# A new hand-written order of all engines in a linear-attention and GEGLU block

## The chip, the cores and the metric

One Trainium2 chip, one of its cores. The time is the device time of one execution in microseconds; the time of the kernel before is the median of three such runs. Beside them stands one execution under the hardware profiler, whose span runs from its first to its last instruction.

## The reference

The input `x` has 2048 rows of 640 numbers in bf16. A layer norm is followed by a linear attention of 32 heads of 20 numbers with learned softmax features, and, after a residual sum, a second layer norm by a gated feed-forward of 1536.

```python
qkv = layernorm(x) @ wqkv                       # heads of 20
pq, pk = q @ w_phi[h], k @ w_phi[h]
phi_q = concat(softmax(pq), softmax(-pq))       # the same for k
kv = einsum("bhsf,bhsd->bhfd", phi_k, v)
z  = phi_k summed over the rows
o  = (phi_q @ kv) / (phi_q @ z + 1e-6)
h  = x + o @ wo
out = h + (gelu(layernorm(h) @ w_gate) * (layernorm(h) @ w_up)) @ w_down
```

## The kernel before, in words

The rows are 16 tiles of 128, in four blocks of four. Tensor engine (TensorE, PE) products run in bf16 into PSUM, which is handed out as four slots of two banks each (`gtile` takes the slot that was given back first, `give` gives it back; both in the order of the program text, so that a call's slot, and the call whose end it must wait for, follow from the order of the calls).

**Every engine executes its instructions in the order in which the calls stand in the list at the end of the kernel** (from line 687 on, 868 calls). The list is written out by hand: each call, such as `km(3)`, issues the instructions of one step for one tile on one engine or two, and the framework adds only the waits that the data, the buffers and the slots need. So a call that waits holds up everything behind it on its own engine. The change touches this list alone. Each of VectorE (DVE), ScalarE (ACT) and GpSimd (POOL) takes the calls that carry its letter, `"v"`, `"a"`, `"g"`; DMAs are all issued by SyncE (SP), in one queue.

The steps, with their lines:

- Start: `warm` and `warms` (L324, L328) are products of zeros, 512 and 128 columns wide. `load_x`, `load_v`, `load_phi`, `load_w` are plain loads; `load_T(i, d)` (L169) loads a 128-column chunk of the q weights (i = 0) or the k weights (i = 1) transposed.
- Layer norm: for tiles 0 to 2 `c_sum` (L226, L228), `c_xc` (x minus its mean, L235), `c_sq`, `c_rstd`; for the others `bn` in two halves (L265, L267), `rt` (reciprocal root, on ACT or POOL), `mr`, and `ap` (L292 on ACT, L294 on DVE), which writes the normalized tile into one of three buffers. `ap(0)`, `ap(1)`, `ap(2)` write these tiles again with their scale, for q.
- Transposed tiles `LN1T`: `tr` (five PE transposes, L151) and `tc_` (copy out of PSUM, L131) for tiles 0 to 5, `dt` (a DMA transpose, L314) for the others and, a second time, for 0 to 2, which may overwrite the tile only when `km` has read it.
- Weights folded with the feature matrix: `bd` makes a block-diagonal matrix BD, `fm(i, d)` (L367) multiplies and `fc` copies (L131).
- v: `vm` (ten products, L341) and `ve` (L348). k: `km` (ten products, L388) and `ke` (two exponentials, L395). `ks` sums an exponential's features over each head (L404), `kr` takes reciprocals (L408), `kx(t, s, e)` multiplies v by them (L414), and `kv(t)` adds 40 small products, 32 columns wide, into the sums `kvp` (L429).
- When all 16 `kv` are in, `kv_mask` (L439, L442) and `kv_clear(5)` make KV. `qm(j)` (L457) and `qe(j, s)` (L461) make q's features for one or two of 20 column groups: j = 0, 1, 2 and 4 to 7 hold two, j = 3 and 8 to 12 one.
- Per tile: `ab` (40 small products, L502), `ae` (copy, L131), `a_den`, `a_rec`, `a_w`, `a_o` (L535, L538), a transpose (`o_tr` and `o_tc` for tiles 0 and 1, `o_dt` for the rest), `po_` (ten products, L557), `res` (residual, L567 or L578), `sq2`, `rt2`, `ap2`, and a transpose (`tr2` and `tc2`, or `dt2`).
- Feed-forward, per block and slice f of 128 of the 1536: `gu` (ten products, L630), `gl` (gelu, L636), `gm` (L643); then per tile `dn` (two halves of 12 products, L655), `da` (L665), `so` (store, L672). Block 0 is done in two halves of 256 columns.

Of the kernel before, what the change touches and what calls it, by code (L numbers as in the profile page):

```python
# [17 lines left out]
def kernel(  # L18
# [667 lines left out]
    nc.scalar.add_instruction(mybir.InstLoadActFuncSet(name=nc.get_next_instruction_name(), act_func_set_id=6))  # L686
    load_x(0, 1)
# [14 lines left out]
    load_x(8, 10)  # L702
    load_x(12, 14)
    load_x(10, 12)
    warm(1, 0)
    warm(0, 1)
    warm(1, 2)
    warm(1, 3)
    warm(1, 4)
    warm(0, 5)  # L710
    warm(1, 6)
    warms(0, 0)
    warms(0, 1)
    warms(1, 2)
    warms(0, 3)
    warms(0, 4)
    warms(0, 5)
    warms(0, 6)
    warms(1, 7)
    warms(0, 8)  # L720
    warms(1, 9)
    warms(0, 10)
    warms(1, 11)
    warm(1, 7)
    warm(1, 8)
    warm(0, 9)
    c_sum(1, "v")
    c_sum(0, "a")
    c_sq(0)
    c_sq(1)  # L730
    c_sum(2, "a")
    c_xc(0)
    tr(0)
    c_xc(1)
    tr(1)
    tc_(0, 0, 2, "v")
    vm(0, 0, 2)
    tc_(0, 2, 5, "v")
    tc_(1, 0, 5, "v")
    vm(1, 0, 2)  # L740
    vm(1, 2, 4)
    c_xc(2)
    tr(2)
    vm(0, 2, 4)
    vm(1, 4, 5)
    vm(0, 4, 5)
    bn(3, 0)
    bn(3, 1)
    tc_(2, 0, 5, "v")
    vm(2)  # L750
    kv_clear(0)
    bd(0, 3, "g")
    kv_clear(1)
    c_rstd(0, 2)
    c_sq(2)
    bd(3, 5, "g")
    rt(3, 1, "a")
    c_rstd(2, 3)
    ve(1)
    ve(0)  # L760
    bn(5, 0)
    ap(3, "v")
    tr(3)
    bn(5, 1)
    rt(5, 1, "g")
    kv_clear(2)
    kv_clear(3)
    warmed()
    tc_(3, 0, 5, "v")
    ve(2)  # L770
    bn(4, 0)
    bn(4, 1)
    fm(1, 0)
    fm(1, 1)
    fc(1, 1, "v")
    fc(1, 0, "a")
    rt(4, 1, "a")
    ap(4, "v")
    vm(3)
    ve(3)  # L780
    fm(1, 2)
    fc(1, 2, "v")
    fm(1, 3)
    fc(1, 3, "a")
    tr(4)
    ap(5, "v")
    tc_(4, 0, 5, "v")
    fm(1, 4)
    loop_pools()
    fc(1, 4, "a")  # L790
    km(0, True)
    ke(0, 0)
    ke(0, 1)
    km(1)
    ke(1, 0)
    km(3)
    ke(3, 0)
    tr(5)
    tc_(5, 0, 5, "a")
    ke(1, 1)  # L800
    km(4)
    ke(4, 0)
    ke(3, 1)
    bn(7, 0)
    bn(7, 1)
    rt(7, 1, "g")
    bn(6, 0)
    bn(6, 1)
    rt(6, 1, "g")
    bn(8, 0, 2)  # L810
    ap(7, "v")
    dt(7)
    bn(9, 0, 2)
    bn(8, 1, 2)
    ap(6, "v")
    dt(6)
    bn(9, 1, 2)
    rt(8, 2, "g")
    mr(8)
    mr(9)  # L820
    ap(9, "a")
    c_late(0, 3)
    kv_clear(4)
    vm(4)
    ke(4, 1)
    km(2)
    ke(2, 0)
    ve(4)
    vm(5, by_chunk=False)
    ve(5)  # L830
    ke(2, 1)
    ks(0)
    bn(10, 0, 2)
    bn(10, 1, 2)
    kr(0)
    bn(11, 0, 2)
    bn(11, 1, 2)
    rt(10, 2, "g")
    mr(11)
    mr(10)  # L840
    ap(10, "a")
    load_w("g", 2, 3)
    load_x(14, 16)
    ks(1)
    bn(12, 0, 2)
    bn(12, 1, 2)
    kr(1)
    kx(0, 1, "g")
    ap(8, "a")
    vm(7, by_chunk=False)  # L850
    vm(6, by_chunk=False)
    ve(7)
    km(5)
    ke(5, 0)
    ve(6)
    km(6)
    ke(6, 0)
    ke(5, 1)
    ke(6, 1)
    kx(1, 0, "g")  # L860
    kx(1, 1, "g")
    km(7)
    ke(7, 0)
    dt(9)
    load_T(0, 1)
    load_T(0, 3)
    vm(9, by_chunk=False)
    ve(9)
    ke(7, 1)
    fm(0, 3)  # L870
    fc(0, 3, "a")
    km(9)
    kv(1)
    bn(13, 0, 2)
    bn(14, 0, 2)
    bn(13, 1, 2)
    rt(12, 2, "g")
    ap(0, "v")
    ks(2)
    kr(2)  # L880
    ks(3)
# [703 lines left out]
```

## Time and profile before

| | us |
|---|---|
| median of 3 runs | 276.25 (275.69 to 276.27) |
| the profiled execution, its own time | 276.97 |
| span of the profiled execution | 275.3 |
| first v product (L341) | 5.86 |
| first k product (L388) | 14.62 |
| first and last visit to the k^T v sums (L429) | 34.70, 70.32 |
| first `ab` | 73.32 |
| first gelu-stage product (L630) | 91.00 |

In the timeline a line gives the start, the length, the engine and line, the operation, the tile written and read, the shape, and the count of like instructions in a row; in brackets stands how long the engine stood idle before it, and what released it. A visit is a run of `kv` calls that follow each other on PE. In the lines by group, the two numbers after the bar are busy time and mean nanoseconds of one instruction. In the chain that ended last, a piece is its start, its length, and what it was.

### The profile page before, as it was taken

How to read it: one execution, taken by the hardware profiler on the slowest of the kernel's cores; microseconds unless marked ns; L12 is line 12 of the kernel's file. 1: busy time of each engine (PE TensorE's matmuls, PEld its weight loads, DVE VectorE, ACT ScalarE, POOL GpSimd, SP SyncE). 2: the span in 40 equal slices, each digit the busy share in tenths (PEclk: the TensorE clock that was granted, in tenths of full speed). 3: DMA queues.
4: the chain of work that ended last, by engine and by line, in shares of the span. 5: the costliest groups of instructions: out<-in, count | busy, mean ns of one | idle time of the engine just before them, and what ended most of it. 6: DMA issues, size and time to landing. Idle time of an engine off the chain costs nothing.

```text
span 275.3 us, 7091 instructions
## 1 busy us (share of the span) xinstructions
PE 268.4 (98%) x2960; PEld 170.6 (62%) x2977; DVE 174.0 (63%) x316; ACT 138.6 (50%) x241; POOL 90.0 (33%) x195
## 2 busy tenths in 40 slices
PE   8999999999999999999999999999999999999995
PEld 3776766765555887788764544675544576444574
DVE  4879999999487777686584764882375412332413
ACT  6888978784798847346614244622123540213200
POOL 4625978988003032155420221450050140000000
PEclk9999999999999999999999999999999999999999
DMA  7957999750460115211412103152000512020012
GB/s 213 183 183 188 165 231 155 125 146 2 143 247 2 26 27 120 50 27 24 73 26 48 29 21 73 26 105 67 0 13 10 74 34 61 14 84 1 0 38 83
DMA packets 43392, 21.62 MB, mean 79 GB/s; under 512 B 35936, under 2 KB 41312, under 8 KB 43360
## 3 DMA queue, kind: packets, MB, share of 16 engines
q1 hardware_dynamic: 43360, 21.17, 34.4%
q8 instruction: 23, 0.38, 0.6%
q14 instruction: 9, 0.07, 0.1%
HBM read 10.18 MB, written 2.62 MB: 47 GB/s over the span
## 4 chain that ended last, share of the span: by engine, by line
PE 82%; DVE 7%; SPq 4%; DMA 4%; issue 1%; POOL 1%; ACT 0%; DVEq 0%
PE gu L630 38%; PE pd L655 19%; PE pq L457 8%; PE po L557 8%; PE pk L388 3%; DVE stats L265 2%; SPq L169 2%; PE ab L502 2%; DMA WqT<-in_A_wqkv_dram 2%; DVE sk L404 2%; DMA x_sb<-in_A_x_dram 2%; PE kvp L429 2%; PE pv L341 1%; DVE ln L294 1%; POOL vt L414 1%
## 5 line engine op out<-in xcount | busy, mean ns | idle before, releaser
L643 DVE TENSOR_TENSOR GT<-gu,g 128x512 bf16<-128x512 f32 (+1 forms) x60 | 33.2, 579 | 50.6 <-ACT g L636 50.4
L636 ACT ACTIVATE g<-gu 128x512 bf16<-128x512 f32 (+1 forms) x60 | 29.4, 510 | 66.4 <-PE gu L630 65.5
L630 PE MATMUL gu<-LN2T,Wg 128*128 128x512 bf16 (+1 forms) x290 | 61.3, 335 | 0.5
L630 PE MATMUL gu<-LN2T,Wu 128*128 128x512 bf16 (+1 forms) x300 | 61.7, 336 | 0.0
L655 PE MATMUL pd<-Wd,GT 128*128 128x320 bf16 (+2 forms) x396 | 54.0, 295 | 0.0
L655 PEld LDWEIGHTS <-GT 128*128 128x128 bf16 x396 | 37.7, 98 | 14.3 <-DVE GT L643 0.3
L630 PEld LDWEIGHTS <-Wu 128*128 128x128 bf16 x300 | 29.4, 98 | 22.6
L630 PEld LDWEIGHTS <-Wg 128*128 128x128 bf16 x300 | 28.8, 98 | 21.3
L414 POOL TENSOR_TENSOR vt<-vS,rs 128x672 bf16<-128x672 bf16 x24 | 33.4, 1417 | 3.7 <-DVE rs L408 3.7
L665 DVE TENSOR_TENSOR y<-pd,x_sb 128x640 bf16<-128x640 f32 (+3 forms) x18 | 13.3, 741 | 23.4 <-PE pd L655 23.4
L535 DVE TENSOR_TENSOR tt<-AB,w 128x1280 bf16<-128x1280 f32 x16 | 24.0, 1498 | 2.3 <-POOL w L529 2.1
L341 PE MATMUL pv<-Wv,LN1T 128*128 128x320 bf16 x160 | 24.0, 299 | 0.3 <-ACT E L395 0.2
L557 PE MATMUL po<-Wo,oT 128*128 128x320 bf16 x160 | 24.0, 299 | 0.0
L388 PE MATMUL pk<-Wk,LN1T 128*128 128x320 bf16 x160 | 23.5, 299 | 0.2 <-DMA LN1T<-ln 0.2
L457 PE MATMUL pq<-LN1T,Wq 128*128 128x512 bf16 x93 | 22.9, 380 | 0.4
L461 ACT ACTIVATE Eq<-pq 128x1024 bf16<-128x1024 f32 (+1 forms) x26 | 20.3, 839 | 5.6 <-PE pq L457 5.5
L404 DVE TENSOR_REDUCE sk<-E 128x64 f32<-128x1280 bf16 x16 | 23.1, 1447 | 0.0
L131 ACT COPY AB<-ab 128x704 f32<-128x704 f32 x21 | 15.1, 744 | 14.4 <-PE ab L502 10.0
L557 PEld LDWEIGHTS <-oT 128*128 128x128 bf16 x160 | 15.6, 98 | 6.9 <-ACT oT L131 0.2
L341 PEld LDWEIGHTS <-LN1T 128*128 128x128 bf16 x160 | 15.2, 98 | 6.9 <-DVE LN1T L131 0.9
L388 PEld LDWEIGHTS <-LN1T 128*128 128x128 bf16 x160 | 15.3, 98 | 6.3 <-DMA LN1T<-ln 0.4
L395 ACT ACTIVATE E<-pk 128x640 bf16<-128x640 f32 x26 | 17.3, 717 | 3.2 <-PE pk L388 3.2
(104 smaller groups left out, 270.9 us busy)
## 6 DMA issues: line engine op xcount, KB each, us to landing
out_dram<-y SPq DMA_DIRECT2D x15, 160.0 KB, 1.9
x_sb<-in_A_x_dram SPq DMA_DIRECT2D x6, 320.0 KB, 4.9
Wg<-in_B_w_gate_dram SPq DMA_DIRECT2D x5, 384.0 KB, 5.6
Wu<-in_B_w_up_dram SPq DMA_DIRECT2D x5, 384.0 KB, 5.3
Wd<-in_B_w_down_dram SPq DMA_DIRECT2D x4, 480.0 KB, 4.5
x_sb<-in_A_x_dram SPq DMA_DIRECT2D x4, 160.0 KB, 3.0
Wv<-in_A_wqkv_dram SPq DMA_DIRECT2D x2, 320.0 KB
Wo<-in_A_wo_dram SPq DMA_DIRECT2D x1, 480.0 KB, 6.5
```

The lines of the kernel that those rows point to most:

```text
L341: nc.tensor.matmul(pv[t][:, u, 0:HD], lhsT=lnT(t, c), rhs=Wv[:, c, u * HD:(u + 1) * HD], start=(c == 0), stop=(c == NC - 1))
L388: nc.tensor.matmul(pk[t][:, u, 0:HD], lhsT=lnT(t, c), rhs=Wk2[:, c, u * HD:(u + 1) * HD], start=(c == 0), stop=(c == NC - 1))
L404: nc.vector.reduce_sum(sk[t], Ek[t].rearrange("p s (h f) -> p (s h) f", f=Dh), axis=AX.X)
L414: E[e].tensor_tensor(Vt[t][:, s], vS[t % 8], rs[t][:, s * H:(s + 1) * H, None].to_broadcast([P, H, VC]), ALU.mult)
L457: nc.tensor.matmul(pqs[j][:, i, :], lhsT=Wq2[:, kc, c * P:(c + 1) * P], rhs=LN1T[b][:, kc, :], start=(kc == 0), stop=(kc == NC - 1))
L461: nc.scalar.activation(Eq[j][:, :, s, :], pqs[j][:, 0:len(QG[j])], ACTF.Exp, scale=(1.0, -1.0)[s])
L535: nc.vector.tensor_tensor(tt.rearrange("p s (h f) -> p s h f", f=Dh), num, w[t][:, :, :, None].to_broadcast([P, 2, H, Dh]), ALU.mult)
L557: nc.tensor.matmul(po[t][:, u, 0:HD], lhsT=oT[t][:, c, :], rhs=Wo[:, c, u * HD:(u + 1) * HD], start=(c == 0), stop=(c == NC - 1))
L630: nc.tensor.matmul(p[:, i, 0:a1 - a0], lhsT=W[:, c, f * P:(f + 1) * P], rhs=LN2T[b][:, c, a0:a1], start=(c == 0), stop=(c == NC - 1))
L636: nc.scalar.activation(x[:, 0:a1 - a0], p[:, 0, 0:a1 - a0], ACTF.Gelu_apprx_tanh)
L643: nc.vector.tensor_tensor(GT[b, f][:, a0:a1], p[:, 1, 0:a1 - a0], x[:, 0:a1 - a0], ALU.mult)
L655: nc.tensor.matmul(pd[k][:, u, n0:n1], lhsT=GT[b, f][:, tl * P:(tl + 1) * P], rhs=Wd[:, f, u * HD + n0:u * HD + n1], start=(f == 0), stop= ...
```

## The change

The list of calls is written anew; the functions stay as they are. Both lists have 868 calls. PE does the same products in both, but for the zeros at the start (seven long and four short before, six and eight after). What differs besides the order is the engine of some calls. For the part up to the last `kv`: on DVE instead of ACT `c_sum(0)`, `c_sum(2)`, `fc(1, 0)`, `fc(0, 4)` and the copy of tile 5; on ACT instead of DVE `c_sum(1)` and the copies of tiles 0, 2, 3 and 4; on DVE instead of POOL `kx(1, 1)`, `kx(8, 0)`, `kx(10, 0)`, `kx(13, 0)` and `bd(3, 5)`; on POOL instead of DVE `kx(2, 0)` and `kx(13, 1)`. Behind it, some `ae`, `a_den` and `a_w` change engines in both directions, and `o_tc(1)` goes from ACT to DVE.

The diff replaces nearly every line of the list. Cut to the parts that matter here, several calls on one line:

```diff
@@ start, warming products and PE's first calls @@
-warm(1, 0) warm(1, 2) warm(1, 3) warm(1, 4) warm(1, 6) warms(1, 2) warms(1, 7) warms(1, 9) warms(1, 11) warm(1, 7) warm(1, 8)
-c_sum(1, "v") c_sum(0, "a") c_sq(0) c_sq(1) c_sum(2, "a") c_xc(0) tr(0) c_xc(1) tr(1)
-tc_(0, 0, 2, "v") vm(0, 0, 2) tc_(0, 2, 5, "v") tc_(1, 0, 5, "v") vm(1, 0, 2) vm(1, 2, 4) c_xc(2) tr(2)
-vm(0, 2, 4) vm(1, 4, 5) vm(0, 4, 5) bn(3, 0) bn(3, 1) tc_(2, 0, 5, "v") vm(2)
...
-ve(1) ve(0) bn(5, 0) ap(3, "v") tr(3) bn(5, 1) rt(5, 1, "g")
...
-fm(1, 0) fm(1, 1) fc(1, 1, "v") fc(1, 0, "a") rt(4, 1, "a") ap(4, "v") vm(3) ve(3) fm(1, 2) fc(1, 2, "v") fm(1, 3) fc(1, 3, "a")
-tr(4) ap(5, "v") tc_(4, 0, 5, "v") fm(1, 4) loop_pools() fc(1, 4, "a") km(0, True)
+warm(1, 0) warm(1, 2) warm(1, 3) warm(1, 4) warm(1, 5) warm(1, 6) warms(1, 0) warms(1, 1) warms(1, 4) warms(1, 5) warms(1, 6)
...
+c_sum(0, "v") c_xc(0) warms(1, 7) warms(1, 8) tr(0) warms(1, 11) c_sum(1, "a") c_sq(0) c_sq(1) c_xc(1) tr(1)
+tc_(1, 0, 5, "v") vm(1, 0, 2) tc_(0, 0, 2, "a") tc_(0, 2, 5, "a") c_rstd(0, 2) vm(0, 0, 2) vm(0, 2, 4) bd(0, 3, "g")
+c_sum(2, "v") c_xc(2) bn(3, 0) bn(3, 1) rt(3, 1, "a") ap(3, "v") warmed() vm(1, 2, 4) vm(1, 4, 5) ve(1) tr(3)
+tc_(3, 0, 5, "a") bd(3, 5, "v") bn(5, 0) bn(5, 1) vm(0, 4, 5) fm(1, 0) fc(1, 0, "v") rt(5, 1, "g") ap(5, "v")
+bn(4, 0) bn(4, 1) tr(2) tc_(2, 0, 5, "a") ve(0) vm(3) fm(1, 2) tr(5) tc_(5, 0, 5, "v") fc(1, 2, "v")
+c_sq(2) c_rstd(2, 3) c_late(0, 3) ve(3) vm(2) ve(2) rt(4, 1, "a") fm(1, 1) fm(1, 3) fc(1, 1, "v") fc(1, 3, "a")
+ap(0, "v") vm(5, by_chunk=False) fm(1, 4) fc(1, 4, "a") km(0, True) ap(4, "v") tr(4)
@@ loop, DVE's and POOL's calls up to the first kv @@
-bn(8, 0, 2) ap(7, "v") dt(7) bn(9, 0, 2) bn(8, 1, 2) ap(6, "v") dt(6) bn(9, 1, 2)
...
-ks(0) bn(10, 0, 2) bn(10, 1, 2) kr(0) bn(11, 0, 2) bn(11, 1, 2)
...
-ks(1) bn(12, 0, 2) bn(12, 1, 2) kr(1) kx(0, 1, "g")
+ap(6, "v") load_x(8, 10) bn(8, 0, 2) bn(9, 0, 2) rt(7, 1, "g") ap(7, "v") bn(9, 1, 2) bn(8, 1, 2) rt(8, 2, "g") mr(9) ks(0) kr(0) kx(0, 0, "g") mr(8)
+load_x(14, 16) load_x(10, 12) bn(10, 0, 2) load_x(12, 14) bn(12, 0, 2) bn(13, 0, 2) bn(13, 1, 2) dt(0) bn(12, 1, 2) kv_clear(0) rt(12, 2, "g")
...
+bn(11, 0, 2) bn(11, 1, 2) bn(10, 1, 2)
...
+ks(1)
...
+bn(14, 0, 2) ap(13, "v")
...
+kr(1) kx(1, 0, "g") kx(1, 1, "v")
...
+kx(0, 1, "g") kv(0) kv(1)
@@ SP's calls in the loop @@
-load_x(6, 8) load_x(8, 10) load_x(12, 14) load_x(10, 12) dt(7) dt(6) load_w("g", 2, 3) load_x(14, 16) dt(9) load_T(0, 1) load_T(0, 3)
-load_w("u", 1, 2) dt(10) dt(8) dt(0) load_T(0, 0) load_w("g", 3, 4) load_w("g", 0, 1) load_w("o", 2, 5) dt(13) dt(12) dt(11)
-load_w("u", 0, 1) load_T(0, 2) dt(14) load_T(0, 4) load_w("o", 0, 2) dt(1) dt(2) dt(15) load_w("g", 4, 5) load_w("u", 3, 4)
+load_x(6, 8) load_x(8, 10) load_x(14, 16) load_x(10, 12) load_x(12, 14) dt(0) dt(6) dt(7) load_T(0, 4) load_w("g", 0, 1) dt(9) dt(8)
+load_T(0, 0) load_w("u", 1, 2) dt(13) dt(10) dt(12) load_w("u", 2, 3) load_T(0, 1) load_T(0, 2) load_T(0, 3) dt(11) load_w("u", 4, 5)
+load_w("o", 2, 5) load_w("g", 4, 5) dt(14) dt(15) load_w("o", 0, 2) load_w("g", 1, 2) load_w("g", 2, 3) load_w("u", 3, 4) dt(1) dt(2)
+load_w("g", 3, 4) load_w("u", 0, 1)
@@ the visits to the sums: what stands between them on PE @@
-kv(1) kv(0) | kv(3) | kv(2) kv(4) | kv(5) kv(6) kv(7) | kv(12) kv(9) kv(10) | kv(8) kv(14) kv(13) | kv(11) kv(15)
+kv(0) kv(1) | kv(2) kv(3) | kv(4) kv(5) kv(7) | kv(9) kv(12) | kv(14) kv(6) kv(13) kv(10) | kv(15) kv(11) kv(8)
@@ the end of the loop @@
-qm(3) qe(3, 0) qe(3, 1) kx(11, 0, "v") kv(11) kx(15, 1, "v") kv(15) kv_mask(0) kv_mask(2) kv_clear(5) qm(4) qe(4, 1)
-ffn_pools() load_w("d", 0, 3) load_w("d", 9, 12) load_w("g", 1, 2) load_w("d", 3, 6) load_w("u", 4, 5) load_w("u", 2, 3) kv_mask(1) ab(0)
+qm(0) qe(0, 0) qe(0, 1) qm(2) qe(2, 1) ks(15) kr(15) kx(15, 0, "v") kx(8, 0, "v") kx(15, 1, "v") kx(8, 1, "g") kv(15) kx(11, 0, "v") kv(11) kv(8)
+kv_mask(0) kv_mask(1) kv_mask(2) ffn_pools() qm(8) qe(2, 0) kv_clear(5) qe(8, 1) ab(0)
@@ the loads of the down weights @@
+ab(4) ae(4, 1, "a") ae(4, 0, "a") a_rec(3) a_w(3, "v") a_o(3) o_dt(2) load_w("d", 3, 6) load_w("d", 6, 9) o_dt(3) load_w("d", 9, 12) load_w("d", 0, 3)
@@ the end @@
-dn(14, 0) da(14, 0, 2) so(14, 0, 640) dn(15, 1, 0, 192) da(15, 1, 2, 0, 192) so(15, 320, 512) dn(15, 1, 192, 320) da(15, 1, 2, 192, 320) so(15, 512, 640)
+dn(14, 0) dn(15, 1, 0, 192) da(14, 0, 2) da(15, 1, 2, 0, 192) so(13, 0, 640) so(14, 0, 640) so(15, 320, 512)
```

More of the change, by code (lines that the diff above doesn't have):

```diff
@@ L1107 @@
     tc2(1, "v")
-    qe(9, 0)
+    a_rec(2)
+    a_w(2, "g")
+    a_o(2)
+    qe(11, 0)
     qm(12)
```

1304 lines of the change are left out of this document (650 added, 654 removed).

## The prediction

> **What bounds the kernel now.** I read the page first, then the waits of TensorE (PE), then the timelines of PE, VectorE (DVE), ScalarE (ACT), GpSimd (POOL) and SyncE (SP), and last the chain that ended last.
>
> ```profile
> span 275.3 us, 7091 instructions
> PE 268.4 (98%) x2960; PEld 170.6 (62%) x2977; DVE 174.0 (63%) x316; ACT 138.6 (50%) x241; POOL 90.0 (33%) x195
> ...
> PE 82%; DVE 7%; SPq 4%; DMA 4%; issue 1%; POOL 1%; ACT 0%; DVEq 0%
> ```
>
> PE is the bound. Its work is the same in both orders, so the change can win only time in which PE stands still, and lose by making it stand still. The waits of PE after its first instruction are these, and from the first gelu product to the last down product there are none:
>
> ```profile
> PE kvp L429 <- POOL vt L414: 0.4, 1, 0.4
> PE wa L367 <- DMA WqT<-in_A_wqkv_dram: 0.4, 1, 0.4
> PE wa L367 <- ACT vS L348: 0.3, 1, 0.3
> PE pk L388 <- DMA LN1T<-ln: 0.2, 1, 0.2
> PE pv L341 <- ACT E L395: 0.2, 1, 0.2
> ```
> ```profile
> 91.00:272.40 181.40, 180.83 (x1606) 113.72 (x1616) 96.71 (x174) 65.47 (x122) 38.19 (x104) 1.00 0.20 43
> ```
>
> That row is of the view by windows: stretch, its length, then the busy time of PE, 180.83 of 181.40. So after 91 us nothing is to be won. What can be won lies in the start and the loop, and it is little.
>
> **The start, step by step.** The timeline of PE up to the first k product (L388), then of DVE and ACT:
>
> ```profile
> 1.24 2.31 PE L324 MATMUL wu<-zero 128*128 128x512 bf16 x5 [1.24 <-DVE zero L679]
> 3.35 0.63 PE L328 MATMUL wu<-zero 128*128 128x128 bf16 x4
> ...
> 5.86 1.92 PE L341 MATMUL pv<-Wv,LN1T 128*128 128x320 bf16 x12
> ...
> 7.90 2.79 PE L341 MATMUL pv<-Wv,LN1T 128*128 128x320 bf16 x18
> 10.52 0.44 PE L151 MATMUL tp<-ident,ln 128*128 128x128 bf16 x5
> 11.24 0.79 PE L367 MATMUL wa<-BD,WkT 128*128 128x140 bf16 x12 [0.28 <-ACT vS L348]
> ...
> 14.62 1.66 PE L388 MATMUL pk<-Wk,LN1T 128*128 128x320 bf16 x11
> ```
> ```profile
> 3.59 0.82 DVE L228 TENSOR_REDUCE tsum<-x_sb 128x1 f32<-128x640 bf16 x1 [1.26 <-DMA x_sb<-in_A_x_dram]
> 7.61 0.89 DVE L265 BATCH_NORM_STATS2 stats<-x_sb 128x6 f32<-128x320 bf16 x2 [0.34 <-DMA x_sb<-in_A_x_dram]
> ...
> 9.56 0.54 DVE L294 TENSOR_SCALAR ln<-x_sb,mv,rstd 128x640 bf16<-128x640 bf16 x1
> ```
> ```profile
> 4.94 0.83 ACT L239 ACTIVATE junk<-x_sb,tsum 128x640 bf16<-128x640 bf16 x1
> ...
> 8.78 0.29 ACT L275 ACTIVATE ve<-mv,eps 128x1 f32<-128x1 f32 x1 [0.69 <-DVE mv L267]
> 9.11 0.20 ACT L276 ACTIVATE rstd<-ve 128x1 f32<-128x1 f32 x1
> ```
>
> A warming product of 512 columns takes 0.42 (five from 1.24 to 3.35), one of 128 takes 0.11, a real one of 320 takes 0.136 (eleven in 1.66, of which the last shows 0.30). In the new order tr(0) stands behind six long and seven short warming products: 1.24 + 2.53 + 0.77 = 4.5. tr(1) ends at 5.7, DVE copies it (0.47) by 6.4, and the first v product runs at 6.45 instead of 5.86. The copies of tile 0 are now on ACT behind one sum and two squares of about 0.95 each, from 3.6 on: 6.4, and 0.35 for the first part, which the v products of tile 1 cover. 18 products are then done at 6.45 + 2.45 = 8.9.
>
> There PE meets tr(3), which is moved ahead of tr(2), of the last chunk of v(0) and of all of v(2). Tile 3 cannot be ready: its x lands at 7.6 (the DVE row that a DMA released), statistics end at 8.75, ACT's Ln and Exp at 9.31, and the normalization on DVE takes 0.45, so tr(3) starts at 9.85. The loads ahead of it on SP keep their places. PE stands still for about 0.95. At 9.85 the new order has 18 products and two transposes behind it; the old one had its 18th at 7.90 + 6 × 0.136 = 8.7 and one transpose (0.28) more: 1.4 behind. The old one then lost 0.28 at 11.24, in truth 0.44, since a product's row lasts 0.16 longer than its slot and hides that much of a wait. **Start: +1.0**, and fm(1,0) to km(0) I find covered after that. Bounds +0.3 (if copies and sums fit closer) and +1.6 (if the copy of tile 3, behind ve(1) on ACT, and fc(1,2), behind four other pieces on DVE, come late too).
>
> **The loop: what goes.** PE's four waits after 14.6 (0.2, 0.4, 0.2, 0.4) are 1.2 by the rows and about 0.16 more each: 1.85. They go because dt(9) to dt(13) and the WqT loads stand earlier on SP, before the bulk of the weight loads: T(0,1) is issued some 8 us ahead of fm(0,1), where the old order had a like product, fm(0, 2), wait for its landing. Moved past the transposes, the weight loads land later, but gate, up and Wo weights are first read at 80 us and after.
>
> ```profile
> 39.08 0.31 PE L429 MATMUL kvp<-vt,E 128*32 128x42 bf16 x20 [0.45 <-POOL vt L414]
> ...
> 62.57 1.14 PE L429 MATMUL kvp<-vt,E 128*32 128x42 bf16 x120
> ...
> 70.32 0.80 PE L429 MATMUL kvp<-vt,E 128*32 128x42 bf16 x80
> 71.05 2.33 PE L457 MATMUL pq<-LN1T,Wq 128*128 128x512 bf16 x9
> ```
>
> The k^T v sums were visited at seven places of PE's order (two calls next to each other are one visit); the new order has six. From start to next start 120 small products take 1.07 and 80 take 0.73, so 40 take 0.34 and 0.05 is left over; the product before a visit holds PE 0.1 longer. A visit less is −0.15. **Loop, what goes: −2.0**; bounds −1.0 (half the waits come back) and −2.0.
>
> **The loop: what comes.** DVE is nearly full from 16.6 to its last product for the sums:
>
> ```profile
> 16.60:69.70 53.10, 51.52 (x892) 35.59 (x894) 51.41 (x76) 41.72 (x67) 41.55 (x49) 1.00 0.70 137
> ```
> ```profile
> 67.27 2.40 DVE L414 TENSOR_TENSOR vt<-vS,rs 128x672 bf16<-128x672 bf16 x3
> 71.21 0.19 DVE L439 TENSOR_SCALAR kvp<-kvp 128x24 f32<-128x24 f32 x1 [1.54 <-PE kvp L429]
> 71.43 0.75 DVE L442 TENSOR_TENSOR KV<-kvp,kmask 128x252 bf16<-128x252 f32 x2
> ```
> ```profile
> L414 POOL TENSOR_TENSOR vt<-vS,rs 128x672 bf16<-128x672 bf16 x24 | 33.4, 1417 | 3.7 <-DVE rs L408 3.7
> ...
> L404 DVE TENSOR_REDUCE sk<-E 128x64 f32<-128x1280 bf16 x16 | 23.1, 1447 | 0.0
> ...
> L414 DVE TENSOR_TENSOR vt<-vS,rs 128x672 bf16<-128x672 bf16 x8 | 7.5, 956 | 0.3
> ...
> L131 DVE CAST Wk<-wa 128x640 bf16<-128x640 f32 x2 | 1.6, 798 | 0.1
> L131 DVE COPY LN1T<-tp 128x640 bf16<-128x640 bf16 x4 | 1.9, 473 | 0.3 <-PE tp L151 0.3
> ...
> LN1T<-ln SPq DMA_TRANSPOSE x13, 3.6
> ```
>
> The new order gives DVE two more products of v by the reciprocals (10 instead of 8: +1.9), one more sum of a tile (+0.8), two more copies of folded weights (+1.6) and a part of BD (not shown on DVE; between nothing and the 0.8 of a copy as large as the sum of a tile; I take the middle, 0.4), and moves the copies of tiles 0, 2, 3 and 4 to ACT and that of tile 5 back (−2.1 + 0.5 = −1.6): **+3.1** before the last visit. ACT is 0.3 lighter. Three places follow.
>
> (1) kv(0) waits for kx(0,1) on POOL, behind kx(1,0), which waits for kr(1). On DVE ks(0) starts at about 22.3: ap(7) takes the buffer of dt(0), which SP may issue only when km(0) has read tile 0 (18.5), and a transpose lands 2 to 3.6 later. Behind ks(0) stand kr(0), eight bn halves (0.45 and, with the aggregation, 0.6 each: 4.1), ks(1), ap(13) and kr(1): about 31.0. Two POOL products of 1.35 end at 33.75, and PE, by its own work from km(0) at 17.0, is there at 33.7: **+0.3** (0 to +1.5).
> (2) The last visit waits for the last DVE product: 69.67 + 3.1, less 0.7 that DVE stands still less before ks(0): 72.1. PE comes there at 70.32 + 2.2 (one more two-block group of q products ahead of it, the 71.05 row) + 1.0 − 2.0 + 0.3 = 71.8: with 0.2 from engine to engine **+0.5** (0 to +2).
> (3) The masks (0.19 and 0.75, from 0.2 after the visit) are covered by one q group of half the size, 1.1 instead of 2.2: **+0.2** (0.1 to 0.5).
>
> **Behind the loop.** The attention tiles keep their work. po_(1) takes the slot that qe(7,1) frees, behind three other Eq activations: **+0.3** (0 to 1). The block changes of the gelu stage have about as much PE work between the last po_ and the first gu as before, where no wait showed: one gu more at the first, two ab fewer at the second, one dn half (12 × 0.136 = 1.6) fewer at the third: 0 (0 to 1.6). At the end two output tiles are written on DVE in the last microsecond, the last piece being 192 columns wide, not 128:
>
> ```profile
> 259.19 13.18 PE pd L655 x108
> 272.39 0.29 DVE y L665
> ```
>
> **+0.1.** Sum: 1.0 − 2.0 + 0.3 + 0.5 + 0.2 + 0.3 + 0.1 = **+0.4**. The profiled execution took 276.97, so 277.4 against its own time; it stood 0.7 above the median of the runs shown, 276.25, so the forecast is **276.7**, own range 276.2 to 277.6.
>
> **Rivals.** *The waits in the loop do not come* (35%): DVE's extra work falls into its idle start, and POOL's product is there in time. The row of masks speaks for it: DVE stood idle 1.54 ahead of them. Then 1.0 − 2.0 + 0.1: 275.35, and 274.65 with the start at its lower bound.
>
> *DVE becomes the bound of the loop* (12%, slower): if nothing of the 3.1 is absorbed and ap(7) and ks waits cost it 1.0, its last product ends at 73.8 and PE waits 2.2 instead of 0.5 at the last visit: 278.4. It decides from about 0.7 more DVE time on. The full window from 16.6 to 69.7 speaks for it, the 1.54 against.
>
> *TensorE stays slow* (8%, slower): the first products of 320 columns ran at the fast rate right at 5.86, after 0.3 without work; now 0.7 without work lies there, from 5.7 to 6.45. If the slow rate (0.42 × 320/512 = 0.26) holds for 18 products, tr(3) comes at 11.2 instead of 9.85: +1.35, 278.0. The rows show only one such step, which is why this is small. [...]
>
> *The last Wd loads come late* (8%, slower): two of the four now stand on SP behind o_dt(3), which waits for a_o(3).
>
> ```profile
> Wd<-in_B_w_down_dram SPq DMA_DIRECT2D x4, 480.0 KB, 4.5
> ```
>
> dn(0,0) is reached at 91.0 + 12 gu of 256 columns (ten products of 0.109 each, 13.0) + 4 ab (0.34 and a switch, 2.0) + 2 po (20 × 0.136, 2.7) = 108.7. With 4.5 to landing and some 1.5 for the second, o_dt(3) must be issued by 102; I find about 101. If DVE is 3 late there, PE waits 2: 278.2.
>
> **How the numbers follow.** Forecast 37%, rivals 35, 12, 8, 8. A measurement of this kernel tells 0.2%, 0.55 us, from no change. Of the first rival 31 points lie under 275.7 and 4 within; of the forecast 13 lie within and 24 above; the rest is above: faster 0.31, same 0.17, slower 0.52. The range runs from the first rival with its bound, 274.7, to the slow rivals with the start at its upper bound, 279.0.
>
> **What would show it.** Start: PE idle before the transpose of tile 3, about 0.95, released by DVE ln; k products from 17.0. Loop: no wait of wa or pk on a DMA; kvp first at 33.7 to 34.2; six visits; the last kx on DVE at 72, and PE waiting for it. After 91: no PE waits; a wait of pd on Wd would be the last rival. It is wrong if PE does not wait before tile 3's transpose, or if the first k product comes before 16.3.

## The result and the profile after

The changed kernel is slower by 0.6%: 278.28 us median of 7 runs (278.11 to 278.57), beside 276.34 for the kernel before on the same chip; the ratio is 1.0061, 95% interval 1.0039 to 1.0082. On another chip it was 277.95 against 276.56, 1.0039 (1.0023 to 1.0054). The forecast was 276.7, slower, in a range of 274.7 to 279.0: the sign and the range hold, the size is 1.6 us short. The profiled execution took 278.24 with a span of 276.5, against 276.97 and 275.3 before. So the traces lie 1.3 apart where the medians lie 1.9 apart: the profiled execution of before stood 0.6 above the median of its runs, which range over 2.0 us, and that of the changed kernel at the median of its own, which range over 0.5. The traces explain the 1.3; why the runs of before differ so much is not known, as one of them alone was profiled.

The page of the changed kernel (span; busy time by engine; chain that ended last by engine), and below it the waits of TensorE (PE), total, count, longest:

```profile
span 276.5 us, 7091 instructions
PE 267.9 (97%) x2963; PEld 171.3 (62%) x2980; DVE 182.1 (66%) x332; ACT 135.1 (49%) x235; POOL 84.2 (30%) x184
...
PE 90%; DVE 4%; DMA 2%; issue 1%; POOL 1%; SPq 1%; ACT 1%; POOLq 0%; DVEq 0%; ACTq 0%
```
```profile
PE tp L151 <- DVE ln L294: 1.1, 1, 1.1
PE kvp L429 <- issue: 0.7, 1, 0.7
PE ab L502 <- ACT AB L131: 0.6, 1, 0.6
PE pv L341 <- DVE LN1T L131: 0.6, 1, 0.6
PE tp L151 <- DVE o L538: 0.3, 1, 0.3
```

All five waits shown for before (on WqT and LN1T by DMA among them) are gone; five others stand there. PE's busy time is the same (268.4 before, 267.9 after), so the difference is made of waits. Where they lie, in PE's timeline of the changed kernel:

```profile
6.26 2.64 PE L341 MATMUL pv<-Wv,LN1T 128*128 128x320 bf16 x18 [0.59 <-DVE LN1T L131]
10.01 0.45 PE L151 MATMUL tp<-ident,ln 128*128 128x128 bf16 x5 [1.10 <-DVE ln L294]
...
17.00 1.52 PE L388 MATMUL pk<-Wk,LN1T 128*128 128x320 bf16 x10
...
33.67 0.83 PE L429 MATMUL kvp<-vt,E 128*32 128x42 bf16 x80
...
54.19 0.67 PE L429 MATMUL kvp<-vt,E 128*32 128x42 bf16 x64
55.60 0.29 PE L429 MATMUL kvp<-vt,E 128*32 128x63 bf16 x16 [0.73 <-issue]
...
71.54 1.14 PE L429 MATMUL kvp<-vt,E 128*32 128x42 bf16 x120
...
73.88 0.59 PE L502 MATMUL ab<-KV,Eq 32*128 32x44 bf16 x40
...
82.17 0.45 PE L151 MATMUL tp<-ident,o 128*128 128x128 bf16 x5 [0.33 <-DVE o L538]
...
90.81 0.71 PE L630 MATMUL gu<-LN2T,Wg 128*128 128x256 bf16 x5
...
108.64 5.06 PE L655 MATMUL pd<-Wd,GT 128*128 128x320 bf16 x36
114.32 0.46 PE L502 MATMUL ab<-KV,Eq 32*128 32x44 bf16 x40 [0.62 <-ACT AB L131]
```

The two timelines are set against each other at points with the same work behind them:

- **First k product:** 17.00, where before had 14.62 and ten products of v (1.36) still to come: +1.02.
- **Last visit:** before began its last two-tile visit at 70.32 and its last product stood at 70.93, with one more q group (ten products, 2.16) to come than the new order: 73.09. After: 72.49. The lead is 0.6, so the loop won 1.6.
- **First gate product:** 18.32 behind the last product of the sums, with `ab(3)` (0.40) still to come; before it was 20.00 (70.93 to 90.93 in the timeline, not quite the 91.00 of the table), less the 2.16 of q products: +0.88 for the attention of the first tiles.
- **Gate stage:** +0.68 at the one `ab` that waits at 114.32. The rest, to the last down product, is +0.15.

1.02 − 1.62 + 0.88 + 0.68 + 0.15 = 1.1, which is what PE's last product is later by (273.24 against 272.13).

VectorE's (DVE's) first sum over features (`ks(0)`), its last products for the sums, and the masks behind them:

```profile
21.43 1.43 DVE L404 TENSOR_REDUCE sk<-E 128x64 f32<-128x1280 bf16 x1
...
67.33 3.65 DVE L414 TENSOR_TENSOR vt<-vS,rs 128x672 bf16<-128x672 bf16 x4
72.76 0.19 DVE L439 TENSOR_SCALAR kvp<-kvp 128x24 f32<-128x24 f32 x1 [1.79 <-PE kvp L429]
```

The products end at 70.98. The `kv(11)` that reads it is the second call of the last visit, 0.36 behind its start, at 71.90: 0.9 to spare.

### The profile page after: what moved, and what is told of

It is laid out like the page before. It is cut to its first block, busy times and chain, and to the rows that moved or that the text cites. A ratio compares the mean times of both kernels' runs of the same rounds, so it can differ in the third digit from the quotient of the medians.

```text
span 276.5 us, 7091 instructions
## 1 busy us (share of the span) xinstructions
PE 267.9 (97%) x2963; PEld 171.3 (62%) x2980; DVE 182.1 (66%) x332; ACT 135.1 (49%) x235; POOL 84.2 (30%) x184
## 4 chain that ended last, share of the span: by engine, by line
PE 90%; DVE 4%; DMA 2%; issue 1%; POOL 1%; SPq 1%; ACT 1%; POOLq 0%; DVEq 0%; ACTq 0%
PE gu L630 38%; PE pd L655 17%; PE pk L388 8%; PE po L557 8%; PE pv L341 7%; PE pq L457 6%; PE kvp L429 2%; PE ab L502 2%; DMA x_sb<-in_A_x_dram 2%; PE wa L367 1%; DVE tt L535 1%; PE tp L151 1%; POOL v L595 1%; SPq L157 0%; DVE o L538 0%
## 5 line engine op out<-in xcount | busy, mean ns | idle before, releaser
L414 POOL TENSOR_TENSOR vt<-vS,rs 128x672 bf16<-128x672 bf16 x22 | 30.8, 1419 | 4.7 <-DVE rs L408 4.6
L395 ACT ACTIVATE E<-pk 128x640 bf16<-128x640 f32 x26 | 17.2, 723 | 2.4 <-issue 1.5
L591 POOL TENSOR_SCALAR v<-sm 128x1 f32<-128x1 f32 x14 | 3.7, 267 | 47.9 <-DVE x_sb L578 45.6
```

The costliest lines, as they stand in the source:

```text
L414: E[e].tensor_tensor(Vt[t][:, s], vS[t % 8], rs[t][:, s * H:(s + 1) * H, None].to_broadcast([P, H, VC]), ALU.mult)
```

## The experiments

Theory: the 1.0 of the start stays, and 1.4 comes from two places that the forecast did not have, the `ab` at 114 and the sums of tile 12. Rivals: VectorE bounds the loop, so that whatever is won ahead of it is lost at the last visit; or the visits themselves cost. Each kernel below differs from the changed one only by the edit shown; kernels of one group ran on one chip beside the kernel before (276.56 for the four e, 276.92 for f and g1, 276.64 for g2, h2 and h4, 276.74 for h5), so between groups the ratios are what compares.

| kernel | us | ratio to before (95%) |
|---|---|---|
| e0_after, unaltered | 277.95 | 1.0039 (1.0023 to 1.0054) |
| e1_start | 277.78 | 1.0040 (1.0026 to 1.0055) |
| e2_ab7 | 277.25 | 1.0018 (1.0001 to 1.0035) |
| e3_loads | 277.38 | 1.0034 (1.0018 to 1.0050) |
| f1_hyb | 279.00 | 1.0094 (1.0061 to 1.0126) |
| f2_otr | 278.16 | 1.0051 (1.0031 to 1.0071) |
| f3_best | 278.90 | 1.0064 (1.0038 to 1.0091) |
| g1_visits | 278.35 | 1.0062 (1.0038 to 1.0085) |
| g2_dve | 278.08 | 1.0047 (1.0029 to 1.0065) |
| h2_start | 277.43 | 1.0028 (1.0015 to 1.0042) |
| h4_all | 276.91 | 1.0014 (1.0000 to 1.0028) |
| h5_three | 276.16 | 0.9984 (0.9968 to 0.9999) |

### The unaltered kernel once more: e0_after

> The changed kernel once more, unaltered. Both theories: span 276.5, waits of PE before the transpose of tile 3 (1.1), in the seventh... in the visit of kv(9) and kv(12) (0.7, no releaser), before ab(7) (0.6). Theory P (a wait of PE costs the end its full length, and each wait has a cause in the order): all three recur in this second execution. Rival Q for the wait in the visit (a chance event of that one execution): it is missing here or stands at another visit.

277.95. The same waits come, of other lengths: 0.4 at the sums of tile 12 instead of 0.7, and in the start 0.6 of the wait for tile 3 moved to a load of Wv. The gap at tile 12 differs by 0.3 between the two executions, and the wait for ln by 0.7; the wait of the `ab` is 0.6 in both.

### The start: e1_start, f1_hyb, h2_start

e1_start puts the two tile-2 calls, and the v products of tiles 0 and 2, ahead of the transpose of tile 3 (and, in the part not shown, `fm(1, 1)` and its copy on VectorE ahead of `fm(1, 2)`):

```diff
+c_sq(2) warmed() tr(2) tc_(2, 0, 5, "a")
 bn(3, 0) bn(3, 1) rt(3, 1, "a") ap(3, "v")
-warmed()
+c_rstd(2, 3)
 vm(1, 2, 4) vm(1, 4, 5)
+vm(0, 4, 5)
 ve(1)
+ve(0) vm(2)
 tr(3)
...
```

> The start alone is put back to what the old order did: tile 2's transpose and v products ahead of tile 3's transpose. Theory P: the 1.1 of idle before tile 3's transpose goes, the first k product comes at about 16.0 instead of 17.0, and the end comes 1.0 earlier: span 275.5. Rival L (the loop is bound by VectorE or ScalarE, and PE only waits in another place): the first k product at 16.0, but new waits of PE between 16 and 72 us take at least half of it, and the last visit starts no earlier than 71.2 (71.54 now): span 276.0 to 276.5.

277.78: nothing that can be told from noise. The wait for ln went, and this came (PE of e1_start):

```profile
14.84 0.47 PE L367 MATMUL wa<-BD,WkT 128*128 128x140 bf16 x6 [0.59 <-DVE Wk L131]
...
16.93 1.52 PE L388 MATMUL pk<-Wk,LN1T 128*128 128x320 bf16 x10
```

The first k product is at 16.93, not 16.0. The transposed tile was only the first of two things that were late: the copies of folded weights on VectorE, which from 9.7 on stands still for hardly 0.3, were next. So "the order of tile 2 and tile 3 costs 1.0" does not hold; the start as VectorE has it costs 1.0.

f1_hyb therefore takes the whole list of the kernel before up to the first exponential (its loads too), and the changed kernel's calls after it:

> The changed kernel with the start of the kernel before put back whole: all engines' order, and the loads, up to the first exponent of the loop, then the calls that remain in the changed kernel's order. (Putting back the two tile-2 calls alone had moved a wait of 0.6 us from the transpose of tile 3 to a product of the combined key weights, released by VectorE, and the first key product stayed at 16.9.) Theory: the start as a whole costs the 1.0 us: the first key product stands at 14.6 to 14.9, the first visit to the sums at 32.5 to 32.9, and the lead holds to the end: 276.9 to 277.1 against 277.95 for the changed kernel. Rival (VectorE bounds the loop, its last product was done only 0.56 us ahead of the last visit): TensorE waits anew ahead of the visits from 54 on, and less than 0.5 is left: 277.5 or more.

279.00, slower than either: it was the second theory, and more. PE of f1_hyb (a second gap, at 50, is shown under e3_loads):

```profile
14.73 1.52 PE L388 MATMUL pk<-Wk,LN1T 128*128 128x320 bf16 x10
...
17.12 1.53 PE L341 MATMUL pv<-Wv,LN1T 128*128 128x320 bf16 x10 [0.59 <-DVE LN1T L131]
...
34.16 0.66 PE L429 MATMUL kvp<-vt,E 128*32 128x42 bf16 x60 [0.32 <-POOL vt L414]
...
56.41 0.28 PE L429 MATMUL kvp<-vt,E 128*32 128x63 bf16 x13 [0.54 <-issue]
...
73.55 0.80 PE L429 MATMUL kvp<-vt,E 128*32 128x42 bf16 x80 [0.46 <-DVE vt L414]
```

The first k product came at 14.73 as the theory had it, but tile 5 was not transposed yet (0.59; the edit's own doing), and in the loop PE waited for products of VectorE and GpSimd (POOL). What made VectorE late is seen in two of its rows; first of the changed kernel, then of f1_hyb, then GpSimd of f1_hyb in the same stretch:

```profile
55.20 0.35 DVE L294 TENSOR_SCALAR ln<-x_sb,tmean,trstd 128x640 bf16<-128x640 bf16 x1
55.46 0.88 DVE L414 TENSOR_TENSOR vt<-vS,rs 128x672 bf16<-128x672 bf16 x1
```
```profile
55.96 1.40 DVE L294 TENSOR_SCALAR ln<-x_sb,tmean,trstd 128x640 bf16<-128x640 bf16 x1
57.29 1.97 DVE L414 TENSOR_TENSOR vt<-vS,rs 128x672 bf16<-128x672 bf16 x1
```
```profile
51.45 7.09 POOL L414 TENSOR_TENSOR vt<-vS,rs 128x672 bf16<-128x672 bf16 x5 [0.69 <-DVE rs L408]
```

The same two VectorE operations took 2.1 longer beside GpSimd's five products. In the changed kernel GpSimd makes masks at that place (eight operations of L198, 55.11 to 57.96). VectorE ends its last product of the loop 2.5 later than in the changed kernel, so these two rows make up most of it. Not every operation grew so: two sums over features at 52.57 of f1_hyb, beside the same five products, took 2.82, where the mean of one is 1.44 in the changed kernel. Why some rows stretch and others do not, no run shows. In these rows the order of the two engines was thus not a sum of durations: who ran beside whom belonged to it.

h2_start is e1_start with one more edit, the copy that had been late moved to ScalarE (ACT): `fc(1, 1, "v")` becomes `fc(1, 1, "a")`.

> The changed kernel with the two tile-2 calls ahead of the transpose of tile 3 again, and one copy of combined key weights (0.77 us) moved from VectorE to ScalarE, for which TensorE had waited 0.59 us once the transpose no longer made it wait. The copy also leaves VectorE's row of work that has no break until 71 us. Theory (the start is held by VectorE's order, and the loop behind it by the length of VectorE's work): the first key product at 16.2 to 16.5, VectorE's last product of the loop near 70.2, TensorE's last visit at 70.4 to 70.7: 277.2 to 277.5 against 277.95. Rival (the statistics of tile 3 on ScalarE or the loads hold the start): the first key product at 16.8 or later, no change.

277.43, in the forecast span, though not by its steps: the first k product stands at 16.70 (16.2 to 16.5 expected; 0.27 was left at a tile copied by VectorE), and in its profiled execution, with a gap of 0.6 at tile 12, the last product of the sums came no earlier than in e0_after (72.0). It is the ratio, 1.0028 against 1.0039, whose intervals overlap, that speaks for a small gain; it is not shown by this run alone.

### The sums of tile 12: e3_loads

At 54.2 PE runs 64 small products one behind the other and then stops for 0.73, with no semaphore to wait for: "issue". Three weight loads are in flight (issued from 47.4 on, the last at 48.4 with 7.5 to landing). e3_loads issues them behind the last loads of the loop:

```diff
 ks(12) ap(2, "v")
-load_w("g", 1, 2) load_w("g", 2, 3) load_w("u", 3, 4)
 kr(12)
...
 load_w("g", 3, 4) load_w("u", 0, 1)
+load_w("g", 1, 2) load_w("g", 2, 3) load_w("u", 3, 4)
```

> Three weight loads (Wg chunks 1 and 2, Wu chunk 3, 1.1 MB) are moved on SP from ahead of dt(1) to behind the last load of the loop, so that the DMA engines are free at 53 to 56 us. Theory F (PE ran out of instructions in the visit of kv(9) and kv(12), because the 16 KB packet of its instruction queue that ran from 53.1 to 54.2 and the one behind it shared the engines with these loads): the wait of 0.7 without a releaser goes or shrinks to under 0.2, span 275.7. Rival K (the wait is for a product on POOL or VectorE that the profile does not name): it stays, since these loads feed none of them: span 276.5.

277.38, 0.57 less by the medians; the ratios, 1.0034 against 1.0039, lie 0.14 us apart and their intervals overlap, so the time alone does not show it. The traces do: the visit has no gap, and the last product of the sums stands 54.6 behind the first k product, where the unaltered kernel has 55.2 and 55.5. In h4_all and h5_three, which have this edit too, it is 54.7 and 54.6; in e1_start, e2_ab7, f2_otr and h2_start, which do not, 55.1 to 55.3. PE of e3_loads:

```profile
54.39 0.83 PE L429 MATMUL kvp<-vt,E 128*32 128x42 bf16 x80
```

The view by windows (stretch, length, PE busy with instructions, clock, share of the DMA engines, GB/s), of the changed kernel and then of e3_loads:

```profile
53.00:54.00 1.00, 1.00 (x12) 1.00 0.90 339
...
54.50:55.00 0.50, 0.37 (x47) 1.00 0.04 12
55.00:55.50 0.50, 0.00 (x0) 1.00 0.05 18
```
```profile
53.00:54.00 1.00, 1.00 (x10) 1.00 0.00 0
...
54.50:55.00 0.50, 0.50 (x76) 1.00 0.00 0
```

Queue q8 moves instructions (the page of the changed kernel: packets, MB, share of the DMA engines):

```profile
q8 instruction: 23, 0.38, 0.6%
```

Each packet has 16,384 bytes. Counting PE's recorded instructions from the start, the gap opens at the same place in all seven kernels that have it at tile 12: with 1,473 or 1,474 behind it. Two kernels have one in the visit before, with 1,217 behind it, 256 fewer; f3_best is one of them although the three loads are moved there. PE's 5,943 instructions, weight loads among them, are 23 times these 256 and a rest, and the queue has 23 packets. PE of f1_hyb, then of f3_best:

```profile
50.12 0.31 PE L429 MATMUL kvp<-vt,E 128*32 128x42 bf16 x19 [0.54 <-issue]
```
```profile
51.10 0.31 PE L429 MATMUL kvp<-vt,E 128*32 128x42 bf16 x19 [0.61 <-issue]
```

The packet ahead of each of the two places, when PE went on behind it (or passed it), how long that was after the packet's end, and the gap:

```
kernel     place  packet (us)      PE goes on  after packet  gap
after      1,473  53.09 to 54.19   55.60       1.41          0.73
e0_after   1,473  52.70 to 53.82   55.12       1.30          0.41
e1_start   1,473  52.62 to 53.74   55.16       1.42          0.37
e2_ab7     1,473  52.85 to 53.95   55.19       1.24          0.37
h2_start   1,473  52.63 to 53.72   55.12       1.40          0.57
f1_hyb     1,473  53.95 to 55.06   56.41       1.35          0.54
f2_otr     1,473  52.94 to 54.06   55.46       1.40          0.42
f1_hyb     1,217  47.84 to 48.80   50.12       1.32          0.54
f3_best    1,217  48.75 to 49.71   51.10       1.39          0.61
g2_dve     1,473  51.88 to 52.89   54.52       1.63          none
g1_visits  1,473  53.53 to 54.63   56.67       2.04          none
h4_all     1,473  49.94 to 51.08   53.94       2.86          none
h5_three   1,473  49.97 to 50.92   54.11       3.19          none
f3_best    1,473  52.27 to 53.41   56.66       3.25          none
e3_loads   1,473  50.19 to 51.27   54.88       3.61          none
```

In all nine gaps PE goes on 1.24 to 1.42 us behind the end of the packet; where the packet ended 1.6 or more ahead, there is none. The loads make the packet late, not long: it starts 3.0 to 4.0 us after PE passed the place 256 instructions earlier in the nine kernels that have the loads in flight there, and 0.9 to 1.6 in the four that do not (e3_loads, f3_best, h4_all, h5_three). The short products then reach the place too soon, as these times have it: 80 of them with their weight loads use up 160 instructions in 0.8 us. That the loads make the gap at tile 12 is shown by taking them away (no gap there in the four kernels without them in flight, one in seven of the nine with them); that they do it by holding up PE's instructions is the author's estimate from these times, with no run that moved a packet alone. What made the packet of the earlier gaps late, and what takes the 1.3 us behind a packet, no run shows.

### The `ab` at 114: e2_ab7

The scaling of tile 3's second layer norm stands on ScalarE ahead of the copy of attention 6 and waits for GpSimd. The changed kernel, by time, of GpSimd, VectorE and ScalarE:

```profile
111.06 1.49 DVE L535 TENSOR_TENSOR tt<-AB,w 128x1280 bf16<-128x1280 f32 x1
111.28 1.40 POOL L595 TENSOR_SCALAR v<-sm,rstd 128x1 f32<-128x1 f32 x1
...
112.72 0.92 ACT L602 ACTIVATE ln<-x_sb,v,rstd 128x640 bf16<-128x640 bf16 x1 [1.80 <-POOL v L595]
113.54 0.72 ACT L131 COPY AB<-ab 128x704 f32<-128x704 f32 x1
```

Before, in the view by groups, the same GpSimd line:

```profile
L595 POOL TENSOR_SCALAR v<-sm,rstd 128x1 f32<-128x1 f32 x14 | 3.7, 267 | 1.4
```

One number per partition, 0.27 us in the mean of 14, takes 1.40 here: it began 0.22 behind a two-input product of VectorE and ended 0.13 behind its end. ScalarE waits for it, the copy stands behind it, and PE's `ab(7)` needs the copy's slot. The edit:

```diff
-ap2(3, "a") dt2(3)
...
 ae(6, 0, "v")
+ap2(3, "a") dt2(3)
```

> One activation, ap2(3), and its transpose dt2(3) are moved behind the two copies of tile 6's attention products, nothing else. Theory P: the 0.6 of idle before ab(7) goes (0.68 counted from start to start), and the end comes 0.7 earlier: span 275.8. Rival: ap2(3) is late next, so that the first gu of columns 256 to 512 waits for LN2T (its transpose landed 1.4 ahead of it before): a wait at about 117 and a span of 276.3 or more.

277.25, 0.7 less (0.6 by the ratios), and PE does not wait (e2_ab7; GpSimd is as slow as it was):

```profile
111.00 1.39 POOL L595 TENSOR_SCALAR v<-sm,rstd 128x1 f32<-128x1 f32 x1
...
113.35 0.46 PE L502 MATMUL ab<-KV,Eq 32*128 32x44 bf16 x40
```

From the first gate product to the last down product it is 181.75 in each of the four kernels with this edit, and 182.43 to 182.48 in the nine without it.

### What a visit costs: g1_visits

```diff
-kv(0) kv(1) km(8)
+kv(0) km(8) kv(1)
...
-kv(9) kv(12) km(15)
+kv(9) km(15) kv(12)
...
-kv(13) kr(11) kx(11, 1, "g") kv(10) qm(0)
+kr(11) kx(11, 1, "g") qm(0) kv(13) kv(10)
```

(and the same at tiles 3 and 5.)

> The changed kernel with five of its six visits to the k^T v sums cut in two by moving a TensorE call of the loop between (eleven visits, the same products). Theory (a visit costs what the switch between full and quarter tiles takes, about 0.15 us, worked out from the visit rows of before): plus 0.6 to 0.9, 278.6 to 278.9 against 277.95. Rival (a visit costs nothing by itself, and fewer of them was worth nothing): 277.9 to 278.1. Third: the burst of short products outruns the supply of instructions, then shorter visits take away the 0.4 us wait at tile 12's sums, and the sum is plus 0.2 to 0.5.

278.35: plus 0.4 by the times, which were taken on two chips, and 0.6 by the ratios, whose intervals overlap; the times fit the third theory but do not settle it. The trace does better. From the first k product to the last product of the sums it is 55.49, beside 54.62 in e3_loads; both have no gap at tile 12. Against the changed kernel less its gap (54.76) it is 0.73. So five visits cost 0.73 to 0.87, and 0.16 of that is a short stop at the place 1,217: 0.11 to 0.17 each.

### VectorE as the bound: g2_dve

```diff
+c_sum(3, "v") c_sum(3, "v")
 ks(11)
```

> The changed kernel with two more reductions of 0.82 us on VectorE in the middle of the loop (sums of a tile that are not used again), 1.64 us in all, ahead of the denominators of tile 11. Theory (VectorE runs without a break from 14 to 71 us and its last product of the loop is ready 0.2 to 0.6 us ahead of TensorE's last visit, so it is at the bound): TensorE waits for vt at one of the last two visits by 1.0 to 1.4 us, and the time is 278.9 to 279.4 against 277.95. Rival (VectorE has room, the loop is TensorE's alone): less than 0.4, no wait for vt.

278.08, far under the forecast of its theory, and the wait came all the same (VectorE's products behind the two sums; then PE):

```profile
64.43 0.85 DVE L414 TENSOR_TENSOR vt<-vS,rs 128x672 bf16<-128x672 bf16 x1
...
67.85 3.64 DVE L414 TENSOR_TENSOR vt<-vS,rs 128x672 bf16<-128x672 bf16 x4
```
```profile
71.55 0.80 PE L429 MATMUL kvp<-vt,E 128*32 128x42 bf16 x80 [0.46 <-DVE vt L414]
```

Of the 1.6 only 0.7 arrived: the last products end at 71.49, against 70.83 in the unaltered kernel of e0_after, because the product at 64.43 took 0.85 where in e0_after, with a product of GpSimd beside it (62.58 to 63.89), it took 1.69. The gap at tile 12 happened not to come, so PE was 0.5 early, and it waited 0.46. VectorE's room at the last visit is this: 0.9 in the first profile, 0.6 in e0_after, 0.1 in e3_loads (its product ends at 71.13, and PE needs it at 71.23). So what PE wins ahead of the visit can be lost there, after 0.6 to 0.9 us, not after 0.2.

### The two projections: f2_otr, and all together: f3_best, h4_all, h5_three

f2_otr puts `po_(0)` ahead of `o_tr(1)`.

> The changed kernel with one call moved: the first output projection of block 0 ahead of the transpose of the second attention output. Theory: TensorE's wait of 0.33 us at that transpose (for VectorE's o) and the sequencing round it go, since 1.36 us of projection stand ahead of it: 277.5 to 277.6 against 277.95. Rival (the wait only moves: the second LayerNorm's transposes need the same VectorE chain and are late by the same): no change, 277.9 to 278.0, with a wait of about 0.4 at the transpose of ln ahead of 90.

278.16, no gain, as the rival has it, though the wait came at another place: the projection that follows the transpose now had nothing between them (f2_otr, PE).

```profile
84.00 1.53 PE L557 MATMUL po<-Wo,oT 128*128 128x320 bf16 x10 [0.66 <-DVE oT L131]
```

f3_best is f1_hyb with the edits of e2_ab7, e3_loads and f2_otr.

> All that was found, together: the start of the kernel before, the statistics of block 3 behind the copies of attention 6, the three weight loads behind the loop's loads, the projection ahead of the transpose; the rest as changed. If the pieces add up: 277.95 less 1.0 (start), 0.7 (the copies), 0.5 (the loads) and 0.4 (the projection) is 275.3 to 275.5, faster than the kernel before (276.56) by 1.1. If VectorE bounds the loop the start's 1.0 is lost again and it stands at 276.1 to 276.4.

278.90 (277.72 to 280.13), far above both forecasts. Its profiled execution, at 280.13 its slowest, inherits f1_hyb's loop (last product of the sums at 75.08, with two waits for VectorE of 1.1 together and a gap of 0.61 without a semaphore), and has 1.07 at a late load of WkT.

h4_all takes h2_start, e2_ab7 and e3_loads, and moves both projections: `po_(0)` ahead of `o_tr(1)`, and `po_(1) res(1, True)` behind `qm(10) qe(10, 1)`.

> That start, and with it the statistics of block 3 behind the copies of attention 6, the three weight loads behind the loop's loads, and both output projections placed so that half a query product stands between the second transpose and its projection; the rest as changed. If the pieces add up: 277.95 less 0.6 (start), 0.7 (copies), 0.5 (supply of instructions), 0.3 to 0.5 (projections) is 275.7 to 275.9 against 276.3 to 276.9 for the kernel before. If VectorE's work of the loop takes one of the pieces back: 276.2 to 276.6.

276.91, above both forecasts. To the last product of the sums (70.95) all was there, 1.05 ahead of e0_after; at the first gate product 0.53 of it was left. The edit at the projections had put in two waits of its own (h4_all, PE):

```profile
82.40 1.24 PE L457 MATMUL pq<-LN1T,Wq 128*128 128x512 bf16 x5 [0.39 <-ACT Eq L461]
...
85.91 2.32 PE L457 MATMUL pq<-LN1T,Wq 128*128 128x512 bf16 x10 [0.52 <-DVE x_sb L567]
```

h5_three is h4_all with the projections left as changed.

> The kernel before this one without its edit at the projections: the start with one copy on ScalarE, the statistics of block 3 behind the copies of attention 6, the three weight loads behind the loop's loads; the rest as changed. Theory (from the first attention to the second LayerNorm the length is VectorE's chain from the attention sums over o, the residual and the statistics to ln, 18.5 us from the last visit's last product to the first gate product in the changed kernel; the edit at the projections put one more wait into it and made it 19.0): the first gate product 18.4 to 18.6 behind the last visit, TensorE's wait of 0.33 at the second transpose is back, and the time is 276.2 to 276.5 where the kernel before stands at 276.6. Rival (the edit was neutral and the missing 0.5 us is lost elsewhere): 276.8 to 277.0 as with the edit.

276.16 against 276.74, ratio 0.9984 (0.9968 to 0.9999): faster than the changed kernel, and by a hair than the one before, from which the interval only just keeps it apart. The span is 274.4, and PE's waits behind the start are these:

```profile
PE tp L151 <- DVE o L538: 0.3, 1, 0.3
PE ab L502 <- PE pq L457: 0.2, 1, 0.2
```

The first k product stands at 16.43, the last of the sums at 71.06, the first gate product 18.28 behind it (19.03 with the edit at the projections).

## Why the prediction was right in its sign and short in its size

- **Start, +1.0: as forecast.** PE stood still 1.10 ahead of tile 3's transpose, released by VectorE's ln, and the first k product came at 17.00, where 17.0 was forecast. That it fits so closely is in part luck: the first v product came 0.2 earlier and the transpose 0.16 later than forecast, and over the other executions of this start the first k product lies between 16.8 and 17.2. And "fm(1,0) to km(0) I find covered after that" was right only as long as PE came late: e1_start took the wait away and found the copies on VectorE behind it. The place was right, the cause only the first of two.
- **Loop, what goes, −2.0: as forecast.** No wait of `wa` or `pk` on a DMA is left. From the first k product to the last product of the sums, at the points with the same work behind them, the loop took 57.11 before (15.98 to 73.09) and 55.49 after; without the gap at tile 12 (0.73) it would be 2.35 shorter. The forecast had left out a wait of 0.27 for a product of VectorE that the list of longest waits does not show.
- **A visit less, −0.15: as forecast;** g1_visits gives 0.11 to 0.17.
- **(1) kv(0), +0.3, and (2) the last visit, +0.5: did not come.** PE reached `kv(0)` at 33.67 and found it ready. VectorE's last product ended at 70.98 where 72.1 was forecast. Nearly 0.9 of these 1.1 lie where the forecast puts "ks(0) at about 22.3": it began at 21.43, beside 21.38 before. The work added to VectorE ahead of its first sums went into time in which it had stood still (1.32 in one piece at 16.64, before); "less 0.7 that DVE stands still less" was too little.
- **(3) masks and the attention, +0.2 and +0.3: came, as 0.88.** The masks cost what was forecast (0.08 ahead of the first `ab` and 0.14 within it), but the 0.3 was put on a slot of `po_(1)`, and that is not where PE stands still: it loses 0.49 at the second `o_tr`, which waits for VectorE's o, and 0.21 at the transposes of the second layer norm. That the chain there runs through VectorE from the attention sums to ln is what f2_otr and h4_all suggest, which moved PE's calls round it and won nothing; no run made that chain shorter.
- **The failed step is "block changes 0" together with the loop's list of what comes:** it has no place for a wait of 0.68 at 114, inside the gate stage, and none of 0.4 to 0.7 at tile 12. e2_ab7 and e3_loads take them away and with them 0.7 and 0.6 by the medians (0.6 and 0.1 by the ratios; 0.68 and 0.5 to 0.9 in the traces). The second was not to be read from the waits of before: there is no semaphore in it. The first could be found only by asking what stands on ScalarE ahead of each copy, call by call, as had been done for PE and VectorE in the start.
- **The rivals.** The waits of the loop did not come, as the first rival has it, but the rest of that rival (nothing in their place) is wrong. *DVE becomes the bound* was given a limit of 0.7 us: measured 0.6 to 0.9 of room; the changed kernel stays under it, f1_hyb and g2_dve go over. *TensorE stays slow*: 0.59 without work lay ahead of the first v products, and 18 of them took 2.64, 0.138 each after the last one's 0.30: the fast rate at once. In f1_hyb twelve took 2.45, 0.65 more than at the fast rate, which is the most that any run here shows; what made them slower, no run shows. *The last Wd loads* were there: the first down product ran at 108.64 (forecast 108.7) with no wait; the price of that rival was mis-added, since a wait of 2 on 276.7 is 278.7, not 278.2.
- **The total:** forecast +0.4 in the trace, measured +1.1 at PE's last product and +1.3 in the time of the profiled execution (278.24, where 277.4 was forecast). Less 0.8 for (1) and (2), more 1.4 for the two waits not seen, and 0.4 more in the attention make up most of the difference, less 0.3 for the wait left out of the loop's gain. The other 0.7 by which the forecast of 276.7 fell short is the step from the trace to the median: it took off 0.7 because the profiled execution of before stood that far above its median, as if the changed kernel's runs would spread the same way. They do not: its profiled execution stands at its median.

## What to carry to other kernels

In a hand-written order, a wait taken from the engine that bounds the kernel can uncover the next one at once, so read what is second before pricing the first: e1_start won nothing (first k product at 16.9), and only with the second copy moved as well did the start get shorter (16.7, 16.3 and 16.4 in the three kernels that have both). Ask at each call that waits what is queued behind it on its own engine, also far from the edit: one activation moved on ScalarE, with the transfer behind it, was worth 0.6 us of the 1.5 by which the best version beats the changed kernel, both by the ratios. Keep loads that nobody needs yet away from the time ahead of a burst of very short instructions: the three moved in e3_loads were worth 0.5 to 0.9 us in the traces, 0.1 by the ratios. And a forecast of a median needs the spread of the runs on both sides: one profiled execution above its median cost this one 0.7.

## What the runs showed of the hardware that was not expected

- PE stood still without a semaphore, as if it had run out of instructions (the author's estimate; no run moved a packet alone): nine gaps of 0.37 to 0.73 us, all at one of two places 256 instructions apart in its order, inside 80 or 120 products that start some 8 ns apart (80 in 0.64 us). PE went on 1.24 to 1.42 us behind the end of a 16,384-byte packet of instructions, which started 3.0 to 4.0 us after PE had passed the place before when loads were in flight (at 339 GB/s in the changed kernel), and 0.9 to 1.6 when they were not.
- VectorE and GpSimd took longer side by side in some rows: 1.40 us instead of 0.27 for one number per partition on GpSimd beside a product of VectorE, and 1.40 instead of 0.35 and 1.97 instead of 0.88 on VectorE beside GpSimd's products. In these three a duration from a row without such a neighbour was too short by 1.05 to 1.13 us.
